# Loading the second channel block early, through retired staging buffers, in a fused S4 and gated-FFN kernel

## The chip, the cores and the metric

The kernel runs on one core of a Trainium2 chip. The metric is the device time of one execution in microseconds (us); lower is better. Before the change the median of 3 runs is 584.97 us (583.7 to 588.05). The profile is of one further execution, which took 586.07 us; its span, from the first to the last instruction, is 584.3 us.

Five engines run their own instruction lists and meet at semaphores: PE (matmuls), DVE, ACT (which loads a table for functions such as SiLU), POOL and SP (here it only starts transfers). POOL and ACT start transfers too. A transfer that SP starts runs on SP's queue, one that POOL starts on POOL's.

## What is computed

```python
x = A_u                                    # 2048 x 512, float32
xn = _layernorm(x)
s = _A_ref(xn, ...)                        # S4: causal convolution over 2048 steps, one kernel K per channel
    # K = einsum("dn,dnl,dn->dl", Cc, exp(dt*A*l), dt*Bc).real     512 channels, 128 states
    # y = irfft(rfft(xn) * rfft(K))[:2048] + xn * Dskip
g = silu(gelu(xn @ w1 + b1) @ w2 + b2)     # FFN, 512 -> 1792 -> 512
return x + s * g
```

## The kernel before, in words

All in float32; the FFN products are made of three matmuls on split operands (high x high, low x high, high x low).

**First part, 0 to about 400 us.** Two jobs are woven together by a list written out by hand, `ORDER` (lines 48 to 124). Each word of it is one step, such as `S.34.0` (a quarter of the second FFN product of step 34), `KL.22.0` (load the small tables `lh` and `rc` that generator step 22 needs) or `UD.18` (store piece 18 of the generated convolution kernel to device memory, `kgd`). The FFN runs in steps of one 128-wide slice of the hidden layer for 512 time steps; its weights w1 and w2 are loaded into a staging pool `stg` (line 310, four buffers of 2 KB per partition) and split into high and low parts by ACT and DVE. Only w slices 0 to 6 and the even ones after use `stg`; the last is number 12. The sum of the FFN's output over the first half of the hidden layer is kept in device memory (`za`) and added in the second half (`z_add`, line 430), then SiLU is applied (line 433, ACT) and the gate is stored (`gd`).

The second list `ORDER` ends with `SL`, `ST` and `KL0`: for channel block 0 of four, load the normalised input as the transform wants it (`raw`, line 826: four transfers, rows of 128 bytes), turn it on chip into `in0` (`side_turn`, line 838), and load the block's convolution kernel rows into `in1` (`kernel_load`, line 847). `side_skip` (line 853, POOL) adds the skip weight Dskip to the first tap of `in1`.

**Middle part, about 400 to 428 us: the change is here.** Lines 1094 to 1121. The last four FFN steps run (`turn`, then the pieces named S and L in a small list, where `S0` to `S3` and `L0` to `L3` are quarters of the last two steps' second product), and between them the first transform stage of block 0 (`F00`, `F01`, `F10`, `F11`): `first_dft` is 64 small matmuls (line 863) into four PSUM banks, `first_out` copies them into `X` (line 869), two by ACT and two by DVE. All four banks are used by each of these groups, so each group waits for the copies of the group before it. Behind each L quarter stand `z_add` (DVE) and `silu` (ACT). Meanwhile SP loads the table `mc` (four transfers), the last `za` rows as `zi`, and `raw` of block 1; POOL turns block 1, and SP then loads block 1's kernel rows. When the last L quarter is done the pools of the FFN close and SP loads the table `tcn`.

**Last part, 428 us to the end.** For each block, eight slots (`slot`): the second transform stage (line 882), the spectral product, the way back (lines 917, 935, 974) and the gating; the first stage of the next block is spread over the even slots (slots 0 and 2 use `in0`, slots 4 and 6 use `in1`). PE sets the pace there.

Each engine has a list of its own, and what stands in it behind a waiting instruction waits too. A tile in a pool with `bufs=2` waits until the readers of the tile two before it are done. The pool `pf` has the buffer `in` twice: `raw1`, `in0_1` and `in1_1` of block 1 share those two.

Of the kernel before, what the change touches and what calls it, by code (L numbers as in the profile page):

```python
# [11 lines left out]
F32 = mybir.dt.float32  # L12
# [83 lines left out]
C.18.0 WS.13.0 A.18.1 R.33 F.34.1 KL.20.0 B.18.1 E.17.0 U.16 F.35.0 UD.16 G.34 F.35.1 C.18.1 E.17.1 H.34  # L96
XL.2 KL.20.1 F.36.0 N.18.0 R.34 G.35 A.19.0 E.17.2 N.18.1 S.32.0 S.32.1 P.3 Z.19 S.32.2 Q.17 S.32.3
B.19.0 U.17 UD.17 S.33.0 C.19.0 H.35 S.33.1 E.18.0 A.19.1 S.33.2 B.19.1 KL.21.0 KL.21.1 E.18.1 S.33.3
S.34.0 C.19.1 S.34.1 E.18.2 N.19.0 A.20.0 S.34.2 N.19.1 ZA.0.1 S.34.3 Z.20 B.20.0 Q.18 C.20.0 F.36.1
ZA.0.3 U.18 UD.18 ZA.0.2 A.20.1 G.36 ZA.0.0 F.37.0 KL.22.0 E.19.0 KL.22.1 F.37.1 E.19.1 B.20.1 H.36  # L100
F.38.0 C.20.1 ZG.0 R.35 A.21.0 R.36 S.35.0 E.19.2 S.35.1 S.35.2 N.20.0 P.3 Z.21 S.35.3 G.37 Q.19 S.36.0
S.36.1 U.19 H.37 UD.19 B.21.0 S.36.2 N.20.1 C.21.0 S.36.3 R.37 A.21.1 F.38.1 P.3 KL.23.0 KL.23.1 ZL.1
S.37.0 P.3 B.21.1 F.39.0 E.20.0 G.38 C.21.1 F.39.1 E.20.1 H.38 A.22.0 E.20.2 F.40.0 N.21.0 N.21.1 R.38
Z.22 Q.20 B.22.0 F.40.1 C.22.0 A.22.1 S.37.1 KL.24.0 B.22.1 E.21.0 S.37.2 U.20 G.39 UD.20 S.37.3 C.22.1
S.38.0 E.21.1 P.3 S.38.1 H.39 P.3 N.22.0 F.41.0 R.39 E.21.2 P.3 S.38.2 F.41.1 Z.23 Q.21 A.23.0 N.22.1 P.3
S.38.3 B.23.0 S.39.0 C.23.0 S.39.1 XL.3 A.23.1 S.39.2 KL.25.0 B.23.1 E.22.0 S.39.3 KL.24.1 U.21 KL.25.1
G.40 UD.21 C.23.1 E.22.1 A.24.0 H.40 F.42.0 E.22.2 G.41 H.41 F.42.1 R.40 Z.24 N.23.0 B.24.0 Q.22 C.24.0
N.23.1 R.41 A.24.1 S.40.0 KL.26.0 S.40.1 S.40.2 U.22 S.40.3 E.23.0 KL.26.1 B.24.1 UD.22 F.43.0 G.42
C.24.1 E.23.1 A.25.0 S.41.0 H.42 E.23.2 S.41.1 N.24.0 S.41.2 ZA.1.0 Z.25 F.43.1 N.24.1 B.25.0 C.25.0
F.44.0 ZA.1.2 ZA.1.1 A.25.1 F.44.1 R.42 KL.27.0 B.25.1 KL.27.1 G.43 Q.23 E.24.0 S.41.3 E.24.1 H.43 F.45.0  # L110
U.23 R.43 G.44 UD.23 F.45.1 ZA.1.3 H.44 E.24.2 ZG.1 F.46.0 R.44 Z.26 Q.24 C.25.1 A.26.0 N.25.0 F.46.1
B.26.0 U.24 C.26.0 N.25.1 UD.24 S.42.0 A.26.1 S.42.1 KL.28.0 KL.28.1 S.42.2 S.42.3 S.43.0 B.26.1 E.25.0
G.45 S.43.1 ZL.2 C.26.1 S.43.2 E.25.1 S.43.3 H.45 A.27.0 E.25.2 S.44.0 N.26.0 S.44.1 N.26.1 R.45 Z.27
Q.25 B.27.0 F.47.0 C.27.0 A.27.1 F.47.1 KL.29.0 U.25 E.26.0 B.27.1 UD.25 G.46 S.44.2 C.27.1 S.44.3 E.26.1
KL.29.1 A.28.0 S.45.0 H.46 E.26.2 N.27.0 S.45.1 S.45.2 G.47 R.46 Z.28 Q.26 H.47 B.28.0 N.27.1 C.28.0
S.45.3 R.47 S.46.0 A.28.1 F.48.0 KL.30.0 S.46.1 B.28.1 E.27.0 KL.30.1 S.46.2 U.26 UD.26 F.48.1 C.28.1
E.27.1 N.28.0 F.49.0 SL N.28.1 E.27.2 A.29.0 F.49.1 B.29.0 Z.29 G.48 C.29.0 Q.27 E.28.0 A.29.1 E.28.1
H.48 S.46.3 KL.31.0 B.29.1 F.50.0 U.27 C.29.1 G.49 UD.27 F.50.1 R.48 H.49 N.29.0 E.28.2 F.51.0 KL.31.1
G.50 N.29.1 A.30.0 R.49 Z.30 Q.28 B.30.0 S.47.0 C.30.0 S.47.1 A.30.1 U.28 S.47.2 E.29.0 B.30.1 UD.28
S.47.3 F.51.1 C.30.1 H.50 E.29.1 N.30.0 F.52.0 N.30.1 E.29.2 A.31.0 F.52.1 R.50 Z.31 G.51 B.31.0 Q.29  # L120
C.31.0 E.30.0 S.48.0 U.29 A.31.1 UD.29 S.48.1 B.31.1 ZA.2.0 S.48.2 C.31.1 S.48.3 ZA.2.1 N.31.0 ZA.2.3
H.51 S.49.0 ZA.2.2 N.31.1 E.30.1 S.49.1 S.49.2 E.30.2 S.49.3 S.50.0 R.51 S.50.1 ZG.2 E.31.0 S.50.2 S.50.3
E.31.1 F.53.0 Q.30 E.31.2 U.30 UD.30 ST F.53.1 Q.31 U.31 UD.31 KL0
"""


# [42 lines left out]
def kernel(  # L169
# [137 lines left out]
    gk = ExitStack()  # L307
    wpa = opened(fa, "wpa", "left")
    wka = opened(fa, "wka", "left")
    stg = opened(fa, "stg", "left", bufs=4)  # L310
    ps1 = opened(fa, "ps1", "left", space=PSUM)
    par = opened(gk, "par", "right")
    pss = opened(gk, "pss", "right", bufs=1, space=PSUM)
# [118 lines left out]
    def silu(t, i):  # L432
        A.activation(fin[t][:, i, :], fin[t][:, i, :], AF.Silu)
# [298 lines left out]
    def skip_load():  # L732
# [67 lines left out]
    def table_load(t, src):  # L800
        w = t.shape[2] if len(t.shape) == 3 else t.shape[2] * t.shape[3]
        for k in range(0, N1, 8):
            d = t[:, k:k + 8]
            SY.dma_start(d.rearrange("p k m -> p (k m)") if len(t.shape) == 3 else d.rearrange("p k a m -> p (k a m)"),
                         src[:, k * w:(k + 8) * w])
# [10 lines left out]
        return SB["psa"].tile([P, 4, P], F32, tag="a", name=name)  # L816


    def side_load(b):
        if b:  # L820
            t = SB["pf"].tile([P, N2, DB], F32, tag="in", name=f"raw{b}", bufs=2)
        else:
            t = wka.tile([P, N2, DB], F32, tag="xh", name="raw0", bufs=2)
        xv = xs.rearrange("(n m) (b g d) -> b g n m d", n=N1, b=NB, g=G)
        for g in range(G):
            SY.dma_start(t[g * N1:(g + 1) * N1], xv[b, g])
        side[b] = t

    def side_turn(b):
        if b:  # L830
            t = SB["pf"].tile([P, DB, N2], F32, tag="in", name=f"in0_{b}", bufs=2)
        else:
            t = wka.tile([P, DB, N2], F32, tag="xl", name="in0_0", bufs=2)
        raw = side[b].rearrange("p m d -> p d m")
        side[b] = [[t[:, :DB // 2], t[:, DB // 2:]]]
        for h in range(2):
            d, r = side[b][0][h], raw[:, h * DB // 2:(h + 1) * DB // 2]
            GP.tensor_copy(d, r) if b else A.copy(d, r)

    def kernel_load(b):  # L840
        if b:
            k = SB["pf"].tile([P, DB, N2], F32, tag="in", name=f"in1_{b}", bufs=2)
            k = [k[:, :DB // 2], k[:, DB // 2:]]
        else:
            k = [wka.tile([P, DB // 2, N2], F32, tag="x", name=f"in1_0_{h}", bufs=2) for h in range(2)]
        for h in range(2):
            SY.dma_start(k[h], kgd[b].rearrange("p (h d m) -> p h d m", h=2, m=N2)[:, h])
        side[b].append(k)
# [245 lines left out]
    with tc.manual_schedule():  # L1094
        SB["spare"] = False
        open_front()
        table_load(SB["mc"], cm)
        turn(NSUB)
        side_skip(0)
        z_load(NTB - 1)  # L1100
        side_load(1)
        turn(NSUB + 1)
        turn(NSUB + 2)
        ffn_gate(*steps[-1])
        ffn_rest(*steps[-1])
        side_turn(1)
        kernel_load(1)
        SB["spare"] = True
        for p in ("S0", "F00", "S1", "S2", "F01", "S3", "L0", "F10", "L1", "F11", "L2", "L3"):
            if p[0] == "F":  # L1110
                k = int(p[1]), int(p[2])
                first_dft(0, *k, range(G))
                first_out(0, *k, (A, A, V, V))
            else:
                second_part(*steps[-2 if p[0] == "S" else -1], int(p[1]))
                if p[0] == "L":
                    z_add(NTB - 1, int(p[1]))
                    silu(NTB - 1, int(p[1]))
        z_store(NTB - 1)
        side_skip(1)  # L1120
        SB["spare"] = False
        fa.close()
        open_mid()
        table_load(SB["tcn"], ct)
        SY.dma_start(SB["gc"], cg[:, :N1])
        for b in range(NB):
            for g in range(8):
                slot(b, g)
        b = NB - 1
# [49 lines left out]
```

## Time and profile before

| | us |
|---|---|
| median of 3 runs | 584.97 (583.7 to 588.05) |
| the profiled execution | 586.07 |
| its span | 584.3 |
| PE busy in the span | 547.8 (94%) |
| DVE, ACT, POOL busy | 465.7, 423.5, 275.3 |

The mean clock that the throttle granted PE over the span is 0.978. In the page's chain of waits (what ended last, followed backwards) PE has 56%, DVE 27%, ACT 8% and "issue", time in which an engine waits for nothing that the profile shows, 4%. In the page's row of the granted clock in 40 slices all are 0.9 or more but three: 0.8 in the slice from 175.3 us, 0.8 in that from 423.6 us and 0.7 in that from 438.2 us. How a row of the views is read stands where it is shown.

### The profile page before, as it was taken

The page shows a single profiled execution, that of the slowest core. Times are in us where ns is not written, and L with a number is a line of the kernel's source. Part 1 is how long each engine was busy: PE and PEld are TensorE (multiplying, and loading weights), DVE is VectorE, ACT ScalarE, POOL GpSimd, SP SyncE. Part 2 cuts the span into 40 slices and gives each one's busy share as a digit, 9 for nine tenths or more (in the row PEclk, how much of TensorE's full clock was granted, in tenths as well). Part 3 has the DMA queues.
Part 4 walks back from the last instruction along what each step waited for, and adds up shares of the span by engine and source line. Part 5 has one row for each costly group of instructions (what it writes and reads, how often), then busy time and mean ns, then how long its engine had stood idle before and what let it go on. Part 6 is the DMA issues. An engine that isn't in the chain of part 4 may idle for free.

```text
span 584.3 us, 17160 instructions
## 1 busy us (share of the span) xinstructions
PE 547.8 (94%) x7194; PEld 441.1 (76%) x7194; DVE 465.7 (80%) x751; ACT 423.5 (72%) x612; POOL 275.3 (47%) x379
## 2 busy tenths in 40 slices
PE   7869999999969999999998999999899999999995
PEld 7547777777747777777776777778788998987882
DVE  6699998899989979999986978990354765856875
ACT  2658878699975999997999998994444566465442
POOL 1646546844585675687544665730050203313423
PEclk9999999999998999999999999999987999999999
DMA  8984522184726466214337152517959274624954
GB/s 192 329 254 132 194 64 94 37 275 152 245 81 233 149 195 234 92 30 170 101 106 230 36 163 60 78 34 233 267 171 197 87 149 80 182 57 109 205 128 108
DMA packets 99506, 86.65 MB, mean 148 GB/s; under 512 B 44803, under 2 KB 88067, under 8 KB 96357
## 3 DMA queue, kind: packets, MB, share of 16 engines
q1 hardware_dynamic: 94368, 65.11, 41.9%
q0 software_dynamic: 3424, 19.93, 9.9%
q8 instruction: 56, 0.92, 0.7%
q10 hardware_dynamic: 1636, 0.53, 0.5%
q14 instruction: 22, 0.17, 0.1%
HBM read 51.99 MB, written 33.55 MB: 146 GB/s over the span
## 4 chain that ended last, share of the span: by engine, by line
PE 56%; DVE 27%; ACT 8%; issue 4%; POOL 2%; DMA 2%; SPq 0%; DVEq 0%; POOLq 0%
PE s L882 10%; PE s L863 6%; PE sa L917 5%; PE f L249 5%; PE z L295 4%; PE f L250 4%; PE f L251 4%; PE z L297 4%; PE z L296 4%; PE kg L653 4%; DVE e L638 3%; PE w L935 3%; DVE e L642 2%; DVE hl L283 2%; DVE ra L606 2%
## 5 line engine op out<-in xcount | busy, mean ns | idle before, releaser
L615 POOL TENSOR_TENSOR mm<-mm,rc 128x32 f32<-128x32 f32 (+4 forms) x150 | 104.8, 699 | 11.8
L295 PE MATMUL z<-w2h,hh 128*128 128x512 f32 x224 | 96.6, 431 | 0.4 <-ACT hh L273 0.4
L249 PE MATMUL f<-xh,w1h 128*128 128x512 f32 x220 | 92.6, 421 | 1.1 <-ACT w1h L227 0.5
L297 PE MATMUL z<-w2h,hl 128*128 128x512 f32 x224 | 88.8, 397 | 0.0
L296 PE MATMUL z<-w2l,hh 128*128 128x512 f32 x224 | 88.4, 395 | 0.0
L251 PE MATMUL f<-xh,w1l 128*128 128x512 f32 x220 | 85.9, 391 | 1.6 <-POOL w1l L232 1.6
L250 PE MATMUL f<-xl,w1h 128*128 128x512 f32 x220 | 85.8, 390 | 0.0
L882 PE MATMUL s<-X,mc 64*64 64x128 f32 x2048 | 64.8, 277 | 0.2 <-DVE t L899 0.2
L899 DVE TENSOR_TENSOR t<-s,uh 128x512 f32<-128x512 f32 x64 | 41.1, 685 | 29.3 <-ACT uh L890 29.0
L612 POOL COPY mm<-rc 128x32 f32<-128x32 f32 x30 | 12.6, 422 | 102.9 <-DVE e L645 94.6
L882 PEld LDWEIGHTS s<-X,mc 64*64 64x64 f32 x2048 | 57.4, 136 | 4.2 <-issue 2.2
L283 DVE TENSOR_TENSOR hl<-hf,hh 128x512 fp32r<-128x512 f32 x56 | 42.5, 764 | 21.3 <-ACT hh L273 21.1
L638 DVE TENSOR_TENSOR e<-mm,ra 128x1024 f32<-128x1024 f32 x32 | 46.2, 1442 | 15.3 <-ACT ra L626 14.9
L249 PEld LDWEIGHTS f<-xh,w1h 128*128 128x128 f32 x220 | 41.6, 189 | 12.3 <-ACT hf L267 2.8
L297 PEld LDWEIGHTS z<-w2h,hl 128*128 128x128 f32 x224 | 42.7, 191 | 10.7 <-DVE hl L283 1.5
L295 PEld LDWEIGHTS z<-w2h,hh 128*128 128x128 f32 x224 | 43.1, 192 | 9.6 <-ACT hh L273 0.8
L251 PEld LDWEIGHTS f<-xh,w1l 128*128 128x128 f32 x220 | 41.3, 188 | 11.2 <-POOL w1l L232 2.5
L267 ACT ACTIVATE hf<-f,b1s 128x512 f32<-128x512 f32 x56 | 38.3, 688 | 14.8 <-PE f L251 12.5
L296 PEld LDWEIGHTS z<-w2l,hh 128*128 128x128 f32 x224 | 42.9, 192 | 7.8
L250 PEld LDWEIGHTS f<-xl,w1h 128*128 128x128 f32 x220 | 41.4, 188 | 7.9 <-DVE xl L382 0.2
L869 ACT COPY X<-s 128x512 f32<-128x512 f32 x56 | 28.9, 597 | 24.6 <-PE s L863 24.6
L623 ACT ACTIVATE ra<-ra 128x1024 f32<-128x1024 f32 x32 | 33.9, 1059 | 16.4 <-DVE ra L606 16.3
(171 smaller groups left out, 1195.6 us busy)
## 6 DMA issues: line engine op xcount, KB each, us to landing
x<-in_A_u_dram SPq DMA_DIRECT2D x16, 256.0 KB
xs<-x SPq DMA_DIRECT2D x16, 256.0 KB
xt_h<-xh POOLq DMA_DIRECT2D x4, 1024.0 KB, 5.8
xt_l<-xl POOLq DMA_DIRECT2D x4, 1024.0 KB, 8.7
kgd<-ko SPq DMA_DIRECT2D x32, 128.0 KB
za<-zo SPq DMA_DIRECT2D x4, 1024.0 KB
xh<-xt_h POOLq DMA_DIRECT2D x4, 1024.0 KB, 5.7
xl<-xt_l POOLq DMA_DIRECT2D x4, 1024.0 KB, 8.7
```

The source lines that it names most:

```text
L249: PE.matmul(p, wh[:, k, :], xh[:, k, :], start=(k == 0), stop=False)
L250: PE.matmul(p, wh[:, k, :], xl[:, k, :], start=False, stop=False)
L251: PE.matmul(p, wl[:, k, :], xh[:, k, :], start=False, stop=(k == KD - 1))
L267: A.activation(hf, pt.pop((v, f)), AF.Gelu_apprx_tanh, bias=b1s[:, f:f + 1])
L283: V.tensor_sub(hl, hf, hh)
L295: PE.matmul(z, hh[:, s], wh, start=(f0 == 0 and f > 0), stop=False)
L296: PE.matmul(z, hh[:, s], wl, start=False, stop=False)
L297: PE.matmul(z, hl[:, s], wh, start=False, stop=(f0 == FA - 1))
L615: GP.tensor_mul(mv[:, :, 0:3:2, w:2 * w], mv[:, :, 0:3:2, 0:w], rc[:, 2 + 2 * i:4 + 2 * i, :].rearrange("p j c -> p c j").unsqueeze(3).to_ ...
L638: V.tensor_mul(e1, m1.unsqueeze(1).to_broadcast([P, 2, CH, N1]), ra[:, :, :, :N1])
L882: PE.matmul(p[ka * 64:(ka + 1) * 64, r, o, :, jj], mc[h, k, ((0, 2), (1, 0))[c][o], :], xf[b][h, c, :, k, :], start=(c == 0), stop=(c == 1 ...
L899: V.tensor_mul(t, p[:, i, :, 1].unsqueeze(1).to_broadcast([P, 2, 2, P]), uh)
```

## The change

Three things move. First, the raw rows of channel block 1 are loaded in the middle of `ORDER`, behind `S.34.0`: a new step `SC` closes the staging pool `stg` and opens a pool `raw` of the same size (8 KB per partition) in its place, and four steps `SL1.0` to `SL1.3` start one transfer each. Second, in the middle part the load of `zi` stands ahead of the table `mc`, the turn of block 1 comes right behind block 0's `side_skip`, the load of block 1's kernel rows follows at once, since `in1_1` now has a buffer of its own, and `side_skip(1)` stands ahead of the L quarters. The table `tcn` has fewer transfers ahead of it in SP's list. Third, the four SiLU pieces A0 to A3 leave their places behind each `z_add`: A0 stands behind L1, that is behind the copies of F10; A1 behind the copies of F11, A2 and A3 at the end.

```diff
-S.34.0 C.19.1 S.34.1 E.18.2 N.19.0 A.20.0 S.34.2 N.19.1 ZA.0.1 S.34.3 Z.20 B.20.0 Q.18 C.20.0 F.36.1
+S.34.0 SC SL1.0 C.19.1 S.34.1 SL1.1 E.18.2 N.19.0 A.20.0 S.34.2 SL1.2 N.19.1 ZA.0.1 S.34.3 SL1.3 Z.20
...
-    stg = opened(fa, "stg", "left", bufs=4)
+    sg = ExitStack()
+    stg = opened(sg, "stg", "left", bufs=4)
...
+    def stage_close():
+        sg.close()
+        SB["raw1"] = opened(fa, "raw", "left").tile([P, N2, DB], F32, name="raw1")
+
+    def side_piece(b, g):
+        t = side.setdefault(b, SB.get("raw1"))
+        SY.dma_start(t[g * N1:(g + 1) * N1], xs.rearrange("(n m) (b g d) -> b g n m d", n=N1, b=NB, g=G)[b, g])
+
     def side_load(b):
...
         for g in range(G):
-            SY.dma_start(t[g * N1:(g + 1) * N1], xv[b, g])
-        side[b] = t
+            side_piece(b, g)
...
         open_front()
+        z_load(NTB - 1)
         table_load(SB["mc"], cm)
         turn(NSUB)
         side_skip(0)
-        z_load(NTB - 1)
-        side_load(1)
+        side_turn(1)
+        kernel_load(1)
         turn(NSUB + 1)
         turn(NSUB + 2)
         ffn_gate(*steps[-1])
         ffn_rest(*steps[-1])
-        side_turn(1)
-        kernel_load(1)
+        side_skip(1)
         SB["spare"] = True
-        for p in ("S0", "F00", "S1", "S2", "F01", "S3", "L0", "F10", "L1", "F11", "L2", "L3"):
+        for p in "S0 F00 S1 S2 F01 S3 L0 F10 L1 A0 F11 A1 L2 L3 A2 A3".split():
...
+            elif p[0] == "A":
+                silu(NTB - 1, int(p[1]))
             else:
                 second_part(*steps[-2 if p[0] == "S" else -1], int(p[1]))
                 if p[0] == "L":
                     z_add(NTB - 1, int(p[1]))
-                    silu(NTB - 1, int(p[1]))
         z_store(NTB - 1)
-        side_skip(1)
```

SP's instructions in the middle part, before; `gd<-zi` stores the gate, `kgd<-ko` the generated kernel, `in<-kgd` loads kernel rows of a block, `mc` and `tcn` are the tables:

```order
L443 DMA gd_69<-zi_4288 128x4x128
L663 DMA kgd_85<-ko_4891 128x256
L663 DMA kgd_85<-ko_4936 128x256
L847 DMA in_0_0_4939<-kgd_82 128x1024
L847 DMA in_0_1_4940<-kgd_82 128x1024
L804 DMA mc<-in_cm_dram 128x1536 x4
L408 DMA zi_4979<-za_73 128x2048
L826 DMA raw_4981<-xs 32x64x32 x4
L847 DMA in_1_5057<-kgd_83 128x1024 x2
L804 DMA tcn<-in_ct_dram 128x1024 x4
```

And the same stretch of SP after the change:

```order
L444 DMA gd_69<-zi_4297 128x4x128
L664 DMA kgd_85<-ko_4900 128x256
L409 DMA zi_4964<-za_73 128x2048
L664 DMA kgd_85<-ko_4945 128x256
L857 DMA in_0_0_4948<-kgd_82 128x1024
L857 DMA in_0_1_4949<-kgd_82 128x1024
L807 DMA mc<-in_cm_dram 128x1536 x4
L857 DMA in_1_4993<-kgd_83 128x1024 x2
L807 DMA tcn<-in_ct_dram 128x1024 x4
```

The load of `zi` has moved up past the last kernel store, block 0's rows and the table; the raw load is gone from here.

ACT's instructions around the groups F01, F10 and F11, before; `X<-s` is a copy of `first_out`, `zi<-zi` a SiLU piece, `uh<-s` the first copy of the last part:

```order
L869 COPY X_5063<-s_0_0_1_1_5111 128x2x32x8
L433 ACT_TABLE_LOAD
L433 ACTIVATE zi_4979<-zi_4979 128x512
L869 COPY X_5063<-s_0_1_0_0_5158 128x2x32x8
L869 COPY X_5063<-s_0_1_0_1_5159 128x2x32x8
L433 ACTIVATE zi_4979<-zi_4979 128x512
L869 COPY X_5063<-s_0_1_1_0_5203 128x2x32x8
L869 COPY X_5063<-s_0_1_1_1_5204 128x2x32x8
L433 ACTIVATE zi_4979<-zi_4979 128x512 x2
L890 COPY uh_0_5346<-s_0_0_5276 128x512
```

And after:

```order
L879 COPY X_5069<-s_0_0_1_1_5117 128x2x32x8
L879 COPY X_5069<-s_0_1_0_0_5163 128x2x32x8
L879 COPY X_5069<-s_0_1_0_1_5164 128x2x32x8
L434 ACT_TABLE_LOAD
L434 ACTIVATE zi_4964<-zi_4964 128x512
L879 COPY X_5069<-s_0_1_1_0_5208 128x2x32x8
L879 COPY X_5069<-s_0_1_1_1_5209 128x2x32x8
L434 ACTIVATE zi_4964<-zi_4964 128x512 x3
L900 COPY uh_0_5350<-s_0_0_5280 128x512
```

The table load and the first SiLU piece no longer stand ahead of the two copies of F10, nor the second ahead of those of F11.

SP's instructions in the middle of `ORDER`, before, where `lh` and `rc` are the small tables of generator steps 21 and 22:

```order
L578 DMA lh_3444<-pcd_80 96x1x128
L584 DMA rc_3446<-recd_76 128x208
L663 DMA kgd_84<-ko_3524 128x256
L578 DMA lh_3540<-pcd_80 96x1x128
L584 DMA rc_3545<-recd_76 128x208
L443 DMA gd_66<-zi_3009 128x4x128
```

And after:

```order
L579 DMA lh_3444<-pcd_80 96x1x128
L585 DMA rc_3446<-recd_76 128x208
L828 DMA raw_3459<-xs 32x64x32 x4
L664 DMA kgd_84<-ko_3533 128x256
L579 DMA lh_3549<-pcd_80 96x1x128
L585 DMA rc_3554<-recd_76 128x208
```

The four raw transfers stand ahead of a kernel store and of the tables of step 22. PE's and DVE's instructions stand in the same order as before.

More of the change, by code (lines that the diff above doesn't have):

```diff
@@ L98 @@
 B.19.0 U.17 UD.17 S.33.0 C.19.0 H.35 S.33.1 E.18.0 A.19.1 S.33.2 B.19.1 KL.21.0 KL.21.1 E.18.1 S.33.3
-S.34.0 C.19.1 S.34.1 E.18.2 N.19.0 A.20.0 S.34.2 N.19.1 ZA.0.1 S.34.3 Z.20 B.20.0 Q.18 C.20.0 F.36.1
-ZA.0.3 U.18 UD.18 ZA.0.2 A.20.1 G.36 ZA.0.0 F.37.0 KL.22.0 E.19.0 KL.22.1 F.37.1 E.19.1 B.20.1 H.36
-F.38.0 C.20.1 ZG.0 R.35 A.21.0 R.36 S.35.0 E.19.2 S.35.1 S.35.2 N.20.0 P.3 Z.21 S.35.3 G.37 Q.19 S.36.0
-S.36.1 U.19 H.37 UD.19 B.21.0 S.36.2 N.20.1 C.21.0 S.36.3 R.37 A.21.1 F.38.1 P.3 KL.23.0 KL.23.1 ZL.1
@@ L103 @@
[L103 to L122, printed above, removed]
@@ L123 @@
-E.31.1 F.53.0 Q.30 E.31.2 U.30 UD.30 ST F.53.1 Q.31 U.31 UD.31 KL0
+S.34.0 SC SL1.0 C.19.1 S.34.1 SL1.1 E.18.2 N.19.0 A.20.0 S.34.2 SL1.2 N.19.1 ZA.0.1 S.34.3 SL1.3 Z.20
+B.20.0 Q.18 C.20.0 F.36.1 ZA.0.3 U.18 UD.18 ZA.0.2 A.20.1 G.36 ZA.0.0 F.37.0 KL.22.0 E.19.0 KL.22.1
+F.37.1 E.19.1 B.20.1 H.36 F.38.0 C.20.1 ZG.0 R.35 A.21.0 R.36 S.35.0 E.19.2 S.35.1 S.35.2 N.20.0 P.3 Z.21
+S.35.3 G.37 Q.19 S.36.0 S.36.1 U.19 H.37 UD.19 B.21.0 S.36.2 N.20.1 C.21.0 S.36.3 R.37 A.21.1 F.38.1 P.3
+KL.23.0 KL.23.1 ZL.1 S.37.0 P.3 B.21.1 F.39.0 E.20.0 G.38 C.21.1 F.39.1 E.20.1 H.38 A.22.0 E.20.2 F.40.0
@@ new lines @@
+N.21.0 N.21.1 R.38 Z.22 Q.20 B.22.0 F.40.1 C.22.0 A.22.1 S.37.1 KL.24.0 B.22.1 E.21.0 S.37.2 U.20 G.39
+UD.20 S.37.3 C.22.1 S.38.0 E.21.1 P.3 S.38.1 H.39 P.3 N.22.0 F.41.0 R.39 E.21.2 P.3 S.38.2 F.41.1 Z.23
+Q.21 A.23.0 N.22.1 P.3 S.38.3 B.23.0 S.39.0 C.23.0 S.39.1 XL.3 A.23.1 S.39.2 KL.25.0 B.23.1 E.22.0 S.39.3
+KL.24.1 U.21 KL.25.1 G.40 UD.21 C.23.1 E.22.1 A.24.0 H.40 F.42.0 E.22.2 G.41 H.41 F.42.1 R.40 Z.24 N.23.0
+B.24.0 Q.22 C.24.0 N.23.1 R.41 A.24.1 S.40.0 KL.26.0 S.40.1 S.40.2 U.22 S.40.3 E.23.0 KL.26.1 B.24.1
@@ new lines @@
+UD.22 F.43.0 G.42 C.24.1 E.23.1 A.25.0 S.41.0 H.42 E.23.2 S.41.1 N.24.0 S.41.2 ZA.1.0 Z.25 F.43.1 N.24.1
+B.25.0 C.25.0 F.44.0 ZA.1.2 ZA.1.1 A.25.1 F.44.1 R.42 KL.27.0 B.25.1 KL.27.1 G.43 Q.23 E.24.0 S.41.3
+E.24.1 H.43 F.45.0 U.23 R.43 G.44 UD.23 F.45.1 ZA.1.3 H.44 E.24.2 ZG.1 F.46.0 R.44 Z.26 Q.24 C.25.1
+A.26.0 N.25.0 F.46.1 B.26.0 U.24 C.26.0 N.25.1 UD.24 S.42.0 A.26.1 S.42.1 KL.28.0 KL.28.1 S.42.2 S.42.3
+S.43.0 B.26.1 E.25.0 G.45 S.43.1 ZL.2 C.26.1 S.43.2 E.25.1 S.43.3 H.45 A.27.0 E.25.2 S.44.0 N.26.0 S.44.1
@@ new lines @@
+N.26.1 R.45 Z.27 Q.25 B.27.0 F.47.0 C.27.0 A.27.1 F.47.1 KL.29.0 U.25 E.26.0 B.27.1 UD.25 G.46 S.44.2
+C.27.1 S.44.3 E.26.1 KL.29.1 A.28.0 S.45.0 H.46 E.26.2 N.27.0 S.45.1 S.45.2 G.47 R.46 Z.28 Q.26 H.47
+B.28.0 N.27.1 C.28.0 S.45.3 R.47 S.46.0 A.28.1 F.48.0 KL.30.0 S.46.1 B.28.1 E.27.0 KL.30.1 S.46.2 U.26
+UD.26 F.48.1 C.28.1 E.27.1 N.28.0 F.49.0 SL N.28.1 E.27.2 A.29.0 F.49.1 B.29.0 Z.29 G.48 C.29.0 Q.27
+E.28.0 A.29.1 E.28.1 H.48 S.46.3 KL.31.0 B.29.1 F.50.0 U.27 C.29.1 G.49 UD.27 F.50.1 R.48 H.49 N.29.0
@@ new lines @@
+E.28.2 F.51.0 KL.31.1 G.50 N.29.1 A.30.0 R.49 Z.30 Q.28 B.30.0 S.47.0 C.30.0 S.47.1 A.30.1 U.28 S.47.2
+E.29.0 B.30.1 UD.28 S.47.3 F.51.1 C.30.1 H.50 E.29.1 N.30.0 F.52.0 N.30.1 E.29.2 A.31.0 F.52.1 R.50 Z.31
+G.51 B.31.0 Q.29 C.31.0 E.30.0 S.48.0 U.29 A.31.1 UD.29 S.48.1 B.31.1 ZA.2.0 S.48.2 C.31.1 S.48.3 ZA.2.1
+N.31.0 ZA.2.3 H.51 S.49.0 ZA.2.2 N.31.1 E.30.1 S.49.1 S.49.2 E.30.2 S.49.3 S.50.0 R.51 S.50.1 ZG.2 E.31.0
+S.50.2 S.50.3 E.31.1 F.53.0 Q.30 E.31.2 U.30 UD.30 ST F.53.1 Q.31 U.31 UD.31 KL0
@@ L775 @@
         "KL0": lambda: kernel_load(0),
+        "SC": lambda: stage_close(),
+        "SL1": lambda g: side_piece(1, g),
     }
@@ L823, in side_load @@
             t = wka.tile([P, N2, DB], F32, tag="xh", name="raw0", bufs=2)
-        xv = xs.rearrange("(n m) (b g d) -> b g n m d", n=N1, b=NB, g=G)
+        side[b] = t
         for g in range(G):
-            SY.dma_start(t[g * N1:(g + 1) * N1], xv[b, g])
-        side[b] = t
+            side_piece(b, g)
     def side_turn(b):
```

## The prediction, made before the changed kernel was run

> **What bounds the kernel now.** I read the granted clock in windows first, then the chain of waits through the middle part, then each engine's timeline there. Windows (start:end, length, busy time of PE, weight loads, DVE, ACT, POOL; the last three columns are granted clock, DMA share, GB/s):
>
> ```profile
> 360.00:400.00 40.00, 39.56 (x468) 30.89 (x467) 32.12 (x40) 36.70 (x41) 18.13 (x21) 1.00 0.39 77
> 400.00:410.00 10.00, 10.00 (x64) 8.13 (x64) 1.23 (x2) 2.64 (x5) 0.47 (x2) 1.00 0.87 298
> 410.00:420.00 10.00, 9.42 (x195) 7.66 (x189) 4.78 (x8) 3.75 (x7) 0.00 (x0) 1.00 1.02 295
> 421.55:428.38 6.83, 6.83 (x80) 5.67 (x84) 2.50 (x4) 2.02 (x4) 2.98 (x2) 0.50 0.50 43
> 435.20:438.62 3.42, 1.90 (x64) 1.59 (x56) 3.33 (x6) 0.59 (x1) 0.71 (x1) 1.00 1.01 393
> 438.62:445.45 6.83, 6.22 (x87) 5.78 (x88) 2.08 (x5) 2.64 (x5) 0.00 (x0) 0.50 1.04 275
> 450.00:535.00 85.00, 85.00 (x2097) 76.17 (x2094) 55.17 (x81) 50.51 (x94) 17.43 (x15) 1.00 0.49 111
> ```
>
> PE is busy 39.56 of the 40 us ahead of the middle part and all 85 us behind it, so what PE saves between them shortens the whole. There, two stretches of 6.83 us have half the clock. The chain (start, us, what):
>
> ```profile
> 416.58 1.94 PE s L863 x64
> 418.52 0.43 PE z L295
> 418.95 0.23 PE z L296
> ...
> 419.42 1.52 issue
> ...
> 421.38 3.58 PE s L863 x62
> ...
> 427.82 2.19 PE s L882 x64
> 430.00 1.94 PE s L863 x64
> ...
> 435.60 1.50 PE s L863 x48
> 437.10 2.13 issue
> 439.23 1.13 PE s L863 x16
> 440.36 3.62 PE s L882 x64
> ...
> 446.67 1.91 PE s L882 x64
> ...
> 452.43 1.98 PE sa L917 x16
> ```
>
> **Stall 1** is the 1.52 us ahead of F11 (the 64 at L863 from 420.94), **stall 2** the 2.13 us inside a group of block 1. Behind each, the same kind of group takes about twice as long (3.58 for 62 against 1.94 for 64; 3.62 against 1.91).
>
> Who holds F11? F10's banks, whose copies came late. Timelines of ACT, DVE and SP's queue (start, us, ..., idle before and releaser):
>
> ```profile
> 418.45 1.28 ACT L433 ACT_TABLE_LOAD   x1 [2.36 <-issue]
> 420.28 1.05 ACT L869 COPY X<-s 128x512 f32<-128x512 f32 x2
> 428.58 0.63 ACT L433 ACTIVATE zi<-zi 128x512 f32<-128x512 f32 x1 [0.65 <-DVE zi L430]
> 415.09 1.29 DVE L869 COPY X<-s 128x512 f32<-128x512 f32 x2 [2.31 <-PE s L863]
> 418.49 0.69 DVE L430 TENSOR_TENSOR zi<-z,zi 128x512 f32<-128x512 f32 x1 [2.11 <-issue]
> 392.27 2.31 SPq L443 DMA_DIRECT2D gd<-zi  x4
> 394.69 5.75 SPq L663 DMA_DIRECT2D kgd<-ko  x2
> 429.35 1.72 SPq L847 DMA_DIRECT2D in<-kgd  x2
> 431.17 3.42 SPq L804 DMA_DIRECT2D tcn<-in_ct_dram  x4
> ```
>
> `z_add` of L0 and SiLU's table load stand ahead of F10's copies on DVE and ACT. Both start at 418.5, though L0's matmuls end before F10 starts (416.58). Both need `zi`. From 400.44, where SP leaves the two `kgd` stores, it starts by the shapes of its list two loads of 0.524 MB, four of 0.786 and `zi` of 1.05, in all 5.24 MB: at the 296 GB/s of the two windows 17.7 us, until 418.1. Stall 1 is the late landing of `zi`.
>
> Stall 2 falls where 48 of 64 matmuls are done; neither trace nor lists name a semaphore there. The DMA share is 1.01, at 393 GB/s. The page's row of a queue that carries instructions (packets, MB):
>
> ```profile
> q8 instruction: 56, 0.92, 0.7%
> ```
>
> PE runs 7194 matmuls and as many weight loads, 14,388, or 257 per packet. Here 64 matmuls with their loads take 1.93 us, so a packet lasts 3.9 us. My reading, which no row shows: PE ran out of instructions, whose packet was behind data. [...]
>
> **The change part by part.**
>
> *`zi` early, SiLU late.* `zi` now waits for the four `gd` stores (392.27 to 394.58), while SP would sit in the `kgd` stores until 400.44 anyway. If they take as long as POOL's `gd` stores,
>
> ```profile
> DMA to landing us min/median/max: 5.2/9.1/9.9
> ```
>
> SP is held to 404.5 at worst, and rows and `mc` come 4 us later. They have the room: F10 wants the rows at 416.58, and `mc`, which with rows and `zi` makes the 5.24 MB, lands at 418.1 to 422.2; it is wanted at about 423.5. Cost 0.
>
> What is late next at F11? F10's copies. DVE's pair of the group before ended at 416.38, its group 1.6 (six matmuls) before 416.58, so the copies take 1.4 from the group's end. L1 covers 0.9 (418.52 to 419.42). F11 waits 0.5, with a semaphore's delay 0.6. That is under both stalls that half clock followed, so the stretch from 421.55 goes too. From 419.42 to 430.00 PE took 10.58; at full clock the work is 1.94 (F11) + 1.6 (L2 and L3: 0.43 and five of 0.23) + 1.91 (L882) = 5.45, with the 0.6 it is 6.05. **Gain 4.5**; bounds 0.9 (half clock stays) and 5.1 (no wait). F11 then ends at 421.9, L3 at 423.5.
>
> A0 with its table load takes 1.28 + 0.63 after F10's ACT copies (end 419.6): 421.5, 0.4 before F11's copies are due. The last `z_add` ends at 424.7 (F11's DVE copies end 423.3, then two of 0.69), A3 at 425.3, and ACT's next copy is due at 425.4. Cost 0; uncovered, 0.6.
>
> [...] Here half clock follows gaps of 1.52 and 2.13; the trace decides. [...]
>
> *The raw rows in the list.* SP at the place where they go, the same load for block 0, and step 22's use:
>
> ```profile
> 272.84 0.31 SPq L584 DMA_DIRECT2D rc<-recd  x1
> 278.00 0.32 SPq L663 DMA_DIRECT2D kgd<-ko  x1
> 279.18 0.63 SPq L578 DMA_DIRECT2D lh<-pcd  x1
> 361.80 6.50 SPq L826 DMA_DIRECT2D raw<-xs  x4
> 295.14 0.39 PE L592 MATMUL ph<-cbs,lh 96*128 96x512 bf16 x1
> ```
>
> Four transfers hold SP 6.5 us, 273.2 to 279.7. Behind them the kernel store comes 1.7 late and `lh` of step 22 about 1, plus the time of the data in front. PE wants that table at 295.14, 16 us after its issue. The staging pool's last split lies far back, so the first transfer should not wait. Block 0's load cost PE at most the 0.44 idle in 360 to 400. Cost 0 to 0.4; I take 0.4.
>
> *Turn, rows, skip.* POOL:
>
> ```profile
> 406.93 0.23 POOL L853 TENSOR_TENSOR in<-in,dsk 128x16 f32<-128x16 f32 x1 [1.01 <-DMA in<-kgd]
> 425.40 3.92 POOL L838 COPY in<-raw 128x1024 f32<-128x1024 f32 x2 [18.24 <-DMA raw<-xs]
> 429.51 3.08 POOL L443 DMA_DIRECT2D gd<-zi  x4 [0.18 <-issue]
> ```
>
> The turn runs from 407 to 411 in POOL's idle time. `gd` now stands behind `side_skip(1)`, which needs block 1's rows: 6.3 MB after 400.44 at 296 GB/s, 421.7. A3 ends at 425.3, so that wait is hidden. Cost 0.
>
> *Data at stall 2.* Before, block 1's rows (1.05 MB), `tcn` (2.1) and `gd` (1.05) start between 429.35 and 434.6: 4.2 MB, 10.7 us at 393 GB/s, until 440. PE dries up at 437.10, in the middle. After, the rows are in; `tcn` and `gd`, 3.15 MB or 8.0 us, start from 423.6 and are done at about 432. PE reaches the same matmul at 423.5 + (437.10 - 427.82 - 0.28 of half clock) = 432.5, where the data ends. Bounds: the stall stays whole (gain 0) or goes. Going, it gives the 9.57 from 437.10 to 446.67 less 0.5 (16 at L863) + 1.91 + 1.98 = 4.4, so 5.2. I take half the stall, 1.1, too short for half clock: **gain 4.1**.
>
> Sum: 586.07 - 4.5 - 4.1 + 0.4 = 577.9, **578**. The profiled execution is 1.1 above the median of 584.97. I don't carry that over: the three runs spread by 4.35, more than the 3.4 that a stretch of half clock costs, so a lower run may be one that missed a stretch, and that can't be gained twice.
>
> **The rivals.**
> 1. *Stall 2 stays, with its half clock.* For it: `tcn` and `gd` still start together, at the same distance from that matmul. 586.07 - 4.5 + 0.4 = 582.0. Chance 0.33.
> 2. *Stall 2 goes altogether*, the data being done in time: 586.07 - 4.5 - 5.2 + 0.4 = 576.8. Chance 0.14.
> 3. *The half clock comes all the same*, for a cause of its own or behind a new gap, such as `mc` late at 423.5. Then only 0.9 and 1.0 of stall are gained: 584.6. Against it: both stretches begin within 2.2 us of the start of the two gaps. Chance 0.10.
> 4. *Slower: the raw load starves the generator.* If a late reader of the staging buffers holds SP at the first raw transfer (273.2), step 22's `lh` waits too. Room: 295.14 - 273.2 - 6.8 of issue - 5.2 of landing = 9.9 us. Each us past it is one of PE, and 3.4 come on top. From 15 us of holding on all gain is lost; at 25 it is 578 + 15.1 + 3.4 = 596.5. Against it: that pool's last weight is split long before. Chance 0.04.
>
> **How the numbers follow.** Forecast 0.39, rivals 0.33, 0.14, 0.10, 0.04. One per cent is about what a measurement can tell; its borders are 579.1 and 590.8. Faster by over 1%: forecast and rival 2, 0.53, less 0.03 for a stall 2 that halves but lands above the border: 0.50. Within: 0.46. Slower: 0.04. The range holds the forecast and rivals 1 and 2, 0.86 less their edges: from 576.8 and to 582.0, each widened by the 1.1 between profile and median, so 575 to 583.
>
> **What would show it.** Right: `z_add` and F10's copies start within 0.2 us of the end of PE's groups; a gap of about 0.6 ahead of F11; clock 1.00 from 418 to 430; from F10's end to the first L882 group 5.0 us instead of 9.3; POOL's turn near 407. A gap of 1.1 or less with clock 1.00 at stall 2 tells the forecast from rival 1. Wrong: raw transfers that start late in the list, a wait of PE for `lh`, a gap over 1.5 us at F11 or the first L882 group.

## The result, and the profile after

| | before | after |
|---|---|---|
| median, us | 585.94 (583.7 to 588.05, 4 runs) | 578.13 (576.92 to 579.09, 4 runs) |
| the profiled execution, us | 586.07 | 578.16 |
| its span, us | 584.3 | 576.4 |
| mean granted clock | 0.978 | 0.989 |

The time is 0.9866 of before (95% interval 0.9822 to 0.991), 7.8 us less. The forecast was 578. Each stall's term has its own verdict below, for the sum came out right with one term wrong.

In the changed file the lines named in the prediction have moved: 863 is now 873, 882 is 892, 917 is 927, 869 is 879, 430 is 431, 433 is 434, 838 is 848. The windows of after (columns as in the prediction):

```profile
260.00:300.00 40.00, 39.34 (x408) 30.28 (x407) 38.06 (x57) 35.21 (x40) 24.79 (x34) 1.00 0.71 163
410.00:420.00 10.00, 10.00 (x207) 8.41 (x205) 5.74 (x7) 3.34 (x7) 2.44 (x4) 1.00 1.01 405
420.00:430.00 10.00, 10.00 (x267) 8.99 (x270) 5.08 (x9) 7.54 (x13) 3.07 (x4) 1.00 0.43 141
430.00:440.00 10.00, 10.00 (x292) 9.30 (x288) 8.81 (x14) 5.40 (x11) 0.00 (x0) 1.00 0.78 121
440.00:450.00 10.00, 10.00 (x280) 9.23 (x280) 7.15 (x11) 5.04 (x10) 0.15 (x1) 1.00 0.31 34
```

By its records PE is busy throughout from 410 to 450 (what waiting is left lies inside a group), and the clock is 1.00 in every window: both stalls and both stretches of half clock are gone. The chain of waits through the same place:

```profile
413.53 2.25 PE s L873 x64
...
417.37 1.94 PE s L873 x64
419.31 0.44 PE z L295
...
420.22 2.53 PE s L873 x64
...
424.33 1.91 PE s L892 x64
...
431.84 1.94 PE s L873 x64
...
437.67 1.91 PE s L892 x64
...
441.52 2.26 PE s L892 x64
```

F11 (420.22) has no gap ahead of it; it takes 2.53 instead of 1.94, so 0.6 of waiting lies inside the group. The group in which stall 2 lay (431.84) takes 1.94. The timelines of SP's queue, POOL, DVE and ACT:

```profile
273.76 5.88 SPq L828 DMA_DIRECT2D raw<-xs  x4
282.84 0.68 SPq L579 DMA_DIRECT2D lh<-pcd  x1
398.15 0.33 SPq L409 DMA_DIRECT2D zi<-za  x1
406.76 5.57 SPq L807 DMA_DIRECT2D tcn<-in_ct_dram  x4
408.04 3.94 POOL L848 COPY in<-raw 128x1024 f32<-128x1024 f32 x2
426.11 3.07 POOL L444 DMA_DIRECT2D gd<-zi  x4 [7.37 <-ACT zi L434]
410.56 1.98 DVE L283 TENSOR_TENSOR hl<-hf,hh 128x512 fp32r<-128x512 f32 x1 [4.75 <-ACT hh L273]
417.41 0.69 DVE L431 TENSOR_TENSOR zi<-z,zi 128x512 f32<-128x512 f32 x1 [0.42 <-PE z L297]
419.42 1.29 DVE L879 COPY X<-s 128x512 f32<-128x512 f32 x2 [1.32 <-PE s L873]
419.33 1.07 ACT L879 COPY X<-s 128x512 f32<-128x512 f32 x2 [2.65 <-PE s L873]
```

`zi` goes out at 398.15 instead of behind the table and the rows; `z_add` (417.41) and the copies of F10 (419.42, 419.33) start right behind PE's groups. One row was not foreseen: `tcn` starts at 406.76, not at 423.6.

To see where the time went, each matmul of before is set against the same matmul of after, since PE runs them in the same order. Start times by matmul number, from the traces' records:

```
matmul   place                        before    after    after - before
 1000    first part                   146.40   146.28    -0.1
 2000    first part, ahead of raw     254.74   255.32    +0.6
 3400    end of the first part        391.61   392.08    +0.5
 3734    F10's group begins           416.52   417.31    +0.8
 4301    slot 4 of block 0            447.44   438.44    -9.0
 5200                                 481.73   473.07    -8.7
 6200                                 521.65   513.01    -8.6
 7190    end                          576.50   568.63    -7.9
```

All of the gain lies between F10 and slot 4 of block 0. Ahead of it after is 0.8 us behind, 0.6 of which is there before the raw rows are loaded, where the change does nothing. Behind it, 1.1 is given back: 0.35 by matmul 4600, all of it in the group at 441.52 (2.26 instead of 1.91), and most of the rest between matmuls 6600 and 7000, where 8.6 of lead become 7.9. The cause of either is not shown.

### The profile page after: what moved, and what is told of

The parts are those of the page before. It is cut to its first block, busy times and chain, and to the rows that moved or that the text cites. A ratio compares the mean times of both kernels' runs of the same rounds, so it can differ in the third digit from the quotient of the medians.

```text
span 576.4 us, 17161 instructions
## 1 busy us (share of the span) xinstructions
PE 544.0 (94%) x7194; PEld 437.9 (76%) x7194; DVE 465.7 (81%) x751; ACT 423.3 (73%) x612; POOL 274.4 (48%) x379
## 4 chain that ended last, share of the span: by engine, by line
PE 56%; DVE 26%; ACT 7%; issue 4%; POOL 3%; DMA 3%; SPq 1%; DVEq 0%; POOLq 0%
PE s L892 9%; PE s L873 6%; PE sa L927 5%; PE f L249 5%; PE z L295 4%; PE f L250 4%; PE f L251 4%; PE z L297 4%; PE z L296 4%; PE kg L654 4%; DVE e L639 3%; PE w L945 3%; DVE e L643 2%; DVE hl L283 2%; DVE ra L607 2%
## 5 line engine op out<-in xcount | busy, mean ns | idle before, releaser
L295 PE MATMUL z<-w2h,hh 128*128 128x512 f32 x224 | 95.3, 425 | 0.4 <-ACT hh L273 0.4
L249 PE MATMUL f<-xh,w1h 128*128 128x512 f32 x220 | 93.8, 426 | 1.0 <-ACT hf L267 0.5
L892 PE MATMUL s<-X,mc 64*64 64x128 f32 x2048 | 63.2, 272 | 0.2 <-DVE t L909 0.2
L283 DVE TENSOR_TENSOR hl<-hf,hh 128x512 fp32r<-128x512 f32 x56 | 43.7, 786 | 21.4 <-ACT hh L273 21.1
L892 PEld LDWEIGHTS s<-X,mc 64*64 64x64 f32 x2048 | 55.8, 133 | 4.1 <-issue 1.9
```

The source lines that it names most:

```text
L249: PE.matmul(p, wh[:, k, :], xh[:, k, :], start=(k == 0), stop=False)
L283: V.tensor_sub(hl, hf, hh)
L295: PE.matmul(z, hh[:, s], wh, start=(f0 == 0 and f > 0), stop=False)
L892: PE.matmul(p[ka * 64:(ka + 1) * 64, r, o, :, jj], mc[h, k, ((0, 2), (1, 0))[c][o], :], xf[b][h, c, :, k, :], start=(c == 0), stop=(c == 1 ...
```

## The experiments

The theories are those of the prediction. For stall 1: `zi` lands late and holds `z_add` and SiLU's table load ahead of F10's copies; against it, that only one of these two counts, or that the half clock has a cause of its own. For stall 2: PE runs out of instructions because their packet is behind data; against it, a stall of another cause, or one that depends on which queue carries the data.

### Stall 1: one edit at a time

**SiLU moved, nothing else** (before, with the new order of the small list):

```diff
-        for p in ("S0", "F00", "S1", "S2", "F01", "S3", "L0", "F10", "L1", "F11", "L2", "L3"):
+        for p in "S0 F00 S1 S2 F01 S3 L0 F10 L1 A0 F11 A1 L2 L3 A2 A3".split():
...
+            elif p[0] == "A":
+                silu(NTB - 1, int(p[1]))
...
-                    silu(NTB - 1, int(p[1]))
```

> The kernel before, with only the four SiLU pieces moved behind the copies. Theory A (stall 1 is the late landing of zi: DVE's z_add of L0 waits for it and stands ahead of DVE's two copies of F10): stall 1 stays at 1 us or more, stall 2 stays, ratio 0.995 to 1.005, about 585 us. Rival B (SiLU and its table load on ACT hold F10's copies): the wait ahead of F11 goes to 0.6 or less and the half clock behind it goes, 4.5 us gained, about 581.4 us.

Measured: 585.17 us, 0.9971 of before (0.9945 to 0.9997). The timelines of PE, DVE and ACT around F11:

```profile
419.20 0.86 PE L863 MATMUL s<-fc,in 32*128 32x64 f32 x6
418.29 0.69 DVE L430 TENSOR_TENSOR zi<-z,zi 128x512 f32<-128x512 f32 x1 [2.05 <-issue]
418.39 1.07 ACT L869 COPY X<-s 128x512 f32<-128x512 f32 x2 [2.45 <-PE s L863]
427.87 3.22 PE L863 MATMUL s<-fc,in 32*128 32x64 f32 x64 [2.15 <-POOL in L838]
```

The window behind the last of these rows:

```profile
428.43:435.26 6.83, 6.83 (x132) 6.71 (x132) 0.00 (x0) 2.54 (x5) 4.49 (x6) 0.50 0.62 173
```

`zi` still lands at 418.3 (DVE), and yet stall 1 is gone: F11 starts at 419.20. So what cost the 1.52 us was ACT's table load and SiLU piece, which stood ahead of ACT's copies and came late with `zi`, not `z_add`. Almost nothing of it shows in the time, because PE now reaches block 1's first stage before POOL has turned its rows: a wait of 2.15 at 427.87, and half clock behind it.

**`zi` ahead of the table, nothing else**:

```diff
         open_front()
+        z_load(NTB - 1)
         table_load(SB["mc"], cm)
...
-        z_load(NTB - 1)
```

> The kernel before, with only the load of zi moved ahead of the table mc. Theory A: zi lands near 402, z_add of L0 starts when its matmuls end, no wait over 0.7 us ahead of F11 though SiLU stands where it stood; that gains 4.5 us. Raw rows, turn and tcn stay late, and PE now comes to them 4 us earlier, so a gap of 1 to 4 us is left behind 430 (code or tcn): 581 to 585 us. Rival B: SiLU still ahead of F10's copies keeps stall 1: 585 us or more.

Measured: 583.64 us, 0.9971 (0.9938 to 1.0005). Its chain:

```profile
420.15 2.55 PE s L863 x64
...
433.29 3.27 issue
436.56 0.67 PE s L863 x16
437.23 3.47 PE s L882 x64
```

Stall 1 is gone here too. Stall 2 comes at the same matmul as before and is longer, 3.27 instead of 2.13. So each edit by itself removes stall 1, and each by itself is worth about 0.3%, which the second interval does not tell from nothing: what stands behind it takes the gain.

**Raw rows early, and neither of the two** (after, with `zi` behind the table again and SiLU in its old places):

```diff
-        z_load(NTB - 1)
         table_load(SB["mc"], cm)
         turn(NSUB)
         side_skip(0)
+        z_load(NTB - 1)
...
-        for p in "S0 F00 S1 S2 F01 S3 L0 F10 L1 A0 F11 A1 L2 L3 A2 A3".split():
+        for p in ("S0", "F00", "S1", "S2", "F01", "S3", "L0", "F10", "L1", "F11", "L2", "L3"):
...
+                    silu(NTB - 1, int(p[1]))
```

> The changed kernel with zi loaded behind the table mc again and SiLU where it was, so only the early raw rows, the early turn, kernel rows and table tcn are left of the change. Theory A: zi lands at about 418 as before, so stall 1 (1.5 us) and its half clock stay, and stall 2 goes: 5.2 us gained, about 580.7 us. Rival C (the raw rows' small pieces on the queue made zi late): stall 1 goes as well, 576 to 578 us.

Measured: 581.54 us, 0.9934 (0.9908 to 0.996). The timelines of DVE and PE at F11:

```profile
417.83 0.69 DVE L431 TENSOR_TENSOR zi<-z,zi 128x512 f32<-128x512 f32 x1 [1.13 <-DMA zi<-za]
420.29 2.45 PE L873 MATMUL s<-fc,in 32*128 32x64 f32 x64 [0.56 <-issue]
```

And the window behind:

```profile
422.90:426.32 3.42, 3.42 (x26) 2.38 (x29) 2.58 (x4) 1.54 (x4) 0.00 (x0) 0.50 0.31 116
```

With the raw rows out of the way `z_add`, which waits for `zi`, starts 0.7 earlier (417.83 against 418.49), and the gap at F11 shrinks from 1.52 to 0.56. Half clock follows all the same. Stall 2 is gone.

**After, less one of the two.** SiLU in its old places, `zi` early (the second half of the diff above alone):

> The changed kernel with the SiLU pieces back behind each z_add. If either of the two edits (zi ahead of the table, SiLU behind the copies) is enough against stall 1, zi lands near 402, the table load runs at about 417.5 in ACT's idle time ahead of F10's end, and nothing is lost: ratio to the kernel before 0.983 to 0.991, about 578 us. If the SiLU order is needed by itself, F11's gap of 1.5 us and a half clock come back: 582 us.

Measured: 578.84 us, 0.9872 (0.9841 to 0.9902). And `zi` behind the table, SiLU late (its first half alone):

> The changed kernel with zi loaded behind the table mc again, SiLU behind the copies. If either edit is enough: z_add of L0 waits for zi until 417.8 to 418.3 on DVE, so F10's DVE copies come at most 0.4 us late, ACT's are in time, the gap ahead of F11 stays under 0.5 us and the time is within 1 us of the changed kernel, 578 to 579 us. If zi's place is needed by itself: gap of over 1 us at F11, half clock, 582 us.

Measured: 577.97 us, 0.9859 (0.9826 to 0.9893). F11 in the chain of the first of these two kernels:

```profile
419.67 2.54 PE s L873 x64
```

And of the second:

```profile
419.82 2.54 PE s L873 x64
```

Neither has a gap ahead of it, and both take about what F11 takes in after. Both intervals hold the 0.9866 of after: beside the early raw rows, one of the two edits is enough, and the other adds nothing that can be measured. Without either, 0.7% less is gained.

### Stall 2: what holds PE

**`tcn` held back** until behind the last `z_add`, by a small write into its buffer, so that its load starts with `gd`, as the prediction had assumed:

```diff
         open_mid()
+        V.memset(SB["tcn"][:, 0:N1:8, :1], 0.0)
         table_load(SB["tcn"], ct)
```

> The changed kernel, with a small DVE write into the table tcn behind the last z_add (tcn's load overwrites it), so that tcn's load starts at about 425, together with the gate's store, as my prediction had assumed. Theory (stall 2 is a packet of PE's instructions behind data): a gap of 1 to 2 us without a semaphore comes back in the second L863 group of block 1, with or without half clock: 579 to 583 us. Rival D (stall 2 has another cause that the change took away): no such gap, at most a wait for tcn itself at the first L917 group: 578 us.

Measured: 581.81 us, 0.9915 (0.9884 to 0.9945). The timelines of SP's queue and PE:

```profile
425.75 2.83 SPq L807 DMA_DIRECT2D tcn<-in_ct_dram  x4
435.95 0.67 PE L873 MATMUL s<-fc,in 32*128 32x64 f32 x16 [2.11 <-issue]
```

The windows ahead of the gap and behind it:

```profile
430.00:434.00 4.00, 3.83 (x136) 3.52 (x127) 2.66 (x4) 1.83 (x4) 0.00 (x0) 1.00 1.01 353
437.29:440.70 3.41, 3.41 (x53) 3.08 (x44) 0.40 (x1) 1.98 (x4) 0.00 (x0) 0.50 0.86 132
```

Stall 2 is back, whole, at the same matmul, with its half clock: by the medians 3.7 us more than after. The time of `tcn`'s transfer decides, and with it rival 1's 582.0 would have come near. It does not cost as much in every execution: two of the five took 578.47 and 579.7 us, at a mean granted clock of 0.990, the other three 581.81 to 582.27, at 0.986 to 0.988.

**The list shifted**: as the one above, with more warm-up matmuls at the start, which puts 16 matmuls and their weight loads ahead of everything:

```diff
-        warm(35)
+        warm(43)
```

> The kernel with tcn held, with 8 more warm-up matmuls at the very start (16 matmul records and 16 weight loads, 32 instructions, ahead of everything else on PE). If stall 2 is a packet of PE's instructions that comes late, it hits the same instruction of PE's list, counted from its start: the gap moves 16 records forward in the group, from 48 of 64 done to 32 of 64 done, 1.5 to 2.5 us long. If it is a wait of that matmul for data or a bank, or of the engine for a time, it stays at 48 of 64 or moves by no such number. The start may be up to 1 us longer.

One profile, 584.95 us. PE at the place:

```profile
433.81 1.12 PE L873 MATMUL s<-fc,in 32*128 32x64 f32 x32
438.04 1.99 PE L873 MATMUL s<-fc,in 32*128 32x64 f32 x32 [3.11 <-issue]
```

The stall now comes with 32 of the 64 done instead of 48: 16 matmuls earlier in the program, as many as were put in front, and again 4174 matmuls are done when PE stops, of 7210 instead of 7194. A wait for data or for another engine would, as was expected of it, have stayed with its matmul. PE stops at a place in its list counted in instructions, which is what a wait for a packet of them looks like. The packets' own records (queue q8 of the traces) say by how much. The two gaps of the kernel with one queue (below) lie 127 matmuls apart, so PE's matmuls are taken to come 127 to a packet here, with as many loads. The packet that begins with matmul 4174 is taken to be asked for when PE enters the one before, at matmul 4047; no row shows when a packet is asked for, and this is the author's assumption. From the traces:

```
kernel                  matmul 4047  packet      matmul 4174  asked to   packet to  PE's
                        starts       starts      starts       packet     matmul     wait
before                  433.25       436.93      439.23       3.68       2.30       2.13
zi ahead only           429.44       434.10      436.56       4.66       2.46       3.26
tcn held                429.98       433.52      435.95       3.54       2.43       2.11
tcn held, list shifted  431.09       435.65      438.04       4.56       2.39       3.11
gd by SP (below)        433.38       435.81      438.23       2.43       2.42       1.00
raw early only          431.01       432.57      434.87       1.56       2.30       0.01
after                   429.48       430.63      433.16       1.15       2.53       none
```

PE goes on 2.3 to 2.5 us after the start of the packet wherever it waited, and it needs 3.7 to 3.9 from the one matmul to the other. Where PE waited, the way between the two matmuls is 3.84 to 3.86 without the wait. So, by an estimate from these rows and under that assumption, a packet may start about 1.4 us after it is asked for (3.85 less 2.3 to 2.5 is 1.4 to 1.55; raw early only, at 1.56, just touches it), and what comes on top is about what PE waits. After stands at 1.15, within 0.4 of that edge.

**Which queue carries the data?** Before, with `gd` stored by SP instead of POOL:

```diff
-            (GP if t == NTB - 1 else SY).dma_start(gd[b]...
+            SY.dma_start(gd[b]...
```

> The kernel before with one edit: the last gate rows are stored by SP instead of POOL, so rows, gate and tcn go through one queue. If stall 2 needs POOL's queue beside SP's (as the run with one queue suggests): the gap at 48 of 64 falls under 0.7 us and its half clock goes, stall 1 stays as it is: ratio 0.991 to 0.996, 581 to 583 us; smaller gaps may come one packet (128 matmuls) later. If any 4 MB of data at that place do it: stall 2 stays at 1.5 us or more, ratio 0.998 to 1.002.

Measured: 586.84 us, 1.001 (0.9985 to 1.0036). Its chain:

```profile
437.23 1.00 issue
438.23 0.67 PE s L863 x16
438.91 3.50 PE s L882 x64
```

The wait halves, to a size between the two that were expected, half clock follows it still, and nothing comes of it in the time. The same edit on the kernel with `tcn` held back:

> The kernel with tcn held, with the gate stored by SP instead of POOL, so that gate and tcn go through one queue, at the same place and with the same bytes. If any data in flight holds up the packet of instructions: a gap of 1 to 2.5 us at 48 of 64 again. If it takes two queues side by side, POOL's among them: no gap, or one under 0.5 us.

One profile, 580.51 us. Its chain:

```profile
431.21 2.10 PE s L873 x64
...
438.23 0.68 issue
...
443.08 0.63 issue
```

The stall at 48 of 64 is gone, and two of 0.68 and 0.63 come one and two packets later, after 4301 and 4428 matmuls. The clock stays 1.00. That two queues at once delay a packet more than one is not shown by this: with one queue the transfers also start later, so that other data is in flight when PE comes to matmul 4047. In the first of these two kernels the packet starts 2.43 after matmul 4047 with one queue alone. What of the delay is the queue and what the moment stays open.

### The turn beside DVE

**The turn ahead of block 0's `side_skip`**, on after:

```diff
-        side_skip(0)
         side_turn(1)
+        side_skip(0)
```

> The changed kernel with POOL's turn of block 1 ahead of side_skip(0), so that it runs at about 400 to 405 and not at 408 to 412. If DVE's last hl subtraction, which took 1.98 us beside the turn instead of 0.69, was slowed by POOL's copy: it falls back to 0.69 and the F01 group, 2.25 us long, to 1.94; the subtraction that then lies beside the copy, near 405, may be slow instead. If the two have nothing to do with each other, 1.98 stays. The time itself moves by 0.3 us at most.

One profile, 578.9 us. POOL, DVE and the chain of this kernel:

```profile
394.29 4.79 POOL L848 COPY in<-raw 128x1024 f32<-128x1024 f32 x2 [7.23 <-ACT hh L273]
411.53 0.69 DVE L283 TENSOR_TENSOR hl<-hf,hh 128x512 fp32r<-128x512 f32 x1 [4.74 <-ACT hh L273]
414.50 1.94 PE s L873 x64
```

The turn ran earlier than expected, from 394.29. With it out of the way DVE's subtraction takes 0.69 again instead of 1.98, and F01's group 1.94 instead of 2.25. The collision is real and costs PE 0.3 us in after, too little to be told in one time; this run was also 0.9 us behind after at matmul 2000, ahead of all that the edit touches. How late the turn falls sets the price: in the two kernels with one edit less than after the subtraction met the turn too, but took only 1.35 and 1.58, and F01's group 1.94. No version measured here is faster than after beyond what the intervals leave open.

## Why the prediction was right, and where it was not

- **Stall 1, gain 4.5: right in size.** From F10's end to the first L892 group it is 419.31 to 424.33, 5.0 us, where before it was 9.3: 4.3 gained. The wait of 0.6 came as said, inside the group, and no half clock followed. The reason was half right: `zi` was late, but `z_add`, which waits for it ahead of DVE's copies, cost nothing; only ACT's pieces ahead of ACT's copies turned it into a stall, and either edit would have done.
- **SiLU's move, cost 0: right.** The table load (1.28 us) and the pieces fit between the copies, and PE is busy for all 10.00 us from 420 to 430.
- **The raw rows in the list, 0 to 0.4, 0.4 taken: 0.** The four transfers held SP 5.88 us and `lh` of step 22 went out at 282.84 instead of 279.18, still 13 us ahead of its use at 295.69. PE was busy 39.34 of the 40 us from 260 to 300; before:

```profile
260.00:300.00 40.00, 39.32 (x407) 30.34 (x406) 38.11 (x57) 34.87 (x41) 24.88 (x33) 1.00 0.42 137
```

- **The turn from 407 to 411, cost 0: right in time (408.04 to 411.98), wrong in cost.** It was asked who waits for POOL, and not what runs beside it. Price 0.3 in after's profile.
- **"Data at stall 2": the step that failed.** It let `tcn` and `gd` start together from 423.6. `tcn` went out at 406.76: its buffer was free by then, and before, by all that the rows show, it had only stood behind block 1's kernel rows in SP's queue. So only `gd`'s 1.05 MB was in flight, the packet came in time (1.15 after matmul 4047, against 3.68 before), and stall 2 went whole: 424.33 to 437.67 is 13.3 us against the 18.85 from 427.82 to 446.67, 5.5 gained for the 4.1 that was taken, close to rival 2's 5.2. The reading that PE ran out of instructions behind data, which no row showed then, held: the shifted list, where the gap moved from 48 of 64 to 32, shows that it is the instructions, and `tcn` held back, with a wait of 2.11 where after has none, that the data in flight decides.
- **The sum.** 586.07 - 4.3 - 5.5 is 576.3; then come 0.3 for the turn, 0.5 that after is behind by the end of the first part, and 1.1 given back later: 578.2, the 578.16 of the profile. The half stall that the forecast kept stood, by chance, for costs that it had not seen.
- **The rivals.** Rival 2 names what happened to stall 2. Rival 1 needed `tcn` late, and came to 581.81 when it was made so. Rival 3 did not come, but with only the raw rows moved half clock followed a gap of 0.56; the forecast's rule, that 0.6 lies under what costs the clock, was not safe. Rival 4: the first raw transfer did not wait.
- **The profile's 1.1 above the median, not carried over: right.** With a fourth run the median before is 585.94, and after's profile agrees with its median.

## What to carry to other kernels

A transfer's start is read from what it waits for, not from its place in the program: where something long stands ahead of it in the queue, ask when its buffer came free, because that is when it can start once the queue is clear: here `tcn` went out at 406.76, not at 423.6. A stall that no semaphore explains, at a time of heavy traffic, can be tested by shifting the instruction list: here 16 matmuls put in front moved it by 16 matmuls, so it was the instructions that were late, and moving the data was the cure. And an edit that removes the first of two stalls in a row shows little while the second stands: 0.3% alone, where the second alone was worth 0.7% and both together 1.3%.

## What the runs showed of the hardware that was not expected

**PE stopped for its instructions.** In the table of packets above PE waited 1.00 to 3.26 us in the kernels whose packet started 2.43 to 4.66 us after matmul 4047, while data was in flight, and 0.01 or not at all where it started 1.56 or 1.15 us after. How far ahead PE holds instructions no row shows. If a packet is asked for where the table takes it to be, PE holds no more than about one packet ahead, and at the 3.7 to 3.9 us that one took there is about 1.4 us to spare: an estimate of the author's from the table.

**The clock was lost after little.** Half clock followed gaps of 0.56 (raw rows early only), 1.00 (`gd` by SP), 1.52 (before) and 2.11 us (`tcn` held), and lasted 3.41 or 6.83; no length of gap alone decided. With `tcn` and `gd` on one queue, gaps of 0.68 and 0.63 did not cost it. Before, PE stood idle for 1.56 ahead of 313.36, and for 0.53 behind it, without losing it (PE's timeline of before):

```profile
313.36 0.38 PE L592 MATMUL ph<-cbs,lh 96*128 96x512 bf16 x1 [1.56 <-DVE ra L606]
```

The window around it:

```profile
312.33:315.75 3.42, 1.86 (x7) 1.23 (x7) 3.42 (x6) 3.34 (x5) 0.00 (x0) 1.00 0.96 319
```

In three other runs the same two gaps did cost it: half clock came at 315.79 with SiLU alone moved, at 317.02 with the list shifted and at 315.61 with the turn first. The first of these, the 3.41 us ahead of the half clock and the half clock itself:

```profile
312.38:315.79 3.41, 1.68 (x7) 1.08 (x7) 3.41 (x6) 3.32 (x6) 0.00 (x0) 1.00 0.91 302
315.79:319.20 3.41, 3.41 (x24) 2.27 (x26) 2.58 (x5) 3.38 (x4) 0.00 (x0) 0.50 1.01 378
```

In before the starts and ends of half clock in the middle (421.55, 428.38, 438.62, 445.45) lie 6.83, 10.24 and 6.83 apart, whole multiples of 3.41. The window of before shown above ends on that same count, 31 of these steps ahead of 421.55, and holds 1.86 of PE's work. In these two rows the clock stayed at 1.00 behind a step with 1.86 of PE's work and fell to 0.50 behind one with 1.68; that it mattered here how the two gaps fell into the steps is the author's estimate. Busy time did not decide everywhere: with only the raw rows moved PE was busy for 2.81 of the 3.41 us ahead of the half clock at 422.90. What else it takes stays open.

**A DVE subtraction beside a POOL copy ended behind it.** Where `hl` (0.69 us when alone) started beside the turn, it ended 0.54 to 0.56 us after the turn's last copy: in after at 412.54 behind 411.98, with SiLU in its old places at 411.68 behind 411.14, with `zi` behind the table at 412.07 behind 411.52. What links the two no row shows.
